# Two chunks' partial sums added at another time, another order of pairs, and earlier starts around a second MLP

## The chip, the cores and the metric

The kernel runs on one core of a Trainium2 chip. The metric is device time in microseconds (us) of one execution, lower is better. All data lie in DRAM at the start and the result is written there.

## The reference, cut to what matters

```python
def _attn_ref(q, k, v):                       # each 8 x 8 x 576 x 64 (batch, head, token, column)
    q_s = softmax(q, axis=-1)
    k_s = softmax(k, axis=2)                  # over the tokens
    kv = np.einsum('bhsd,bhse->bhde', k_s, v)
    return np.einsum('bhsd,bhde->bhse', q_s, kv)

def _moe_ref(x, w_in, w_out):                 # x 4608 x 512, w_in 512 x 2048, w_out 2048 x 512
    h = x @ w_in
    return np.maximum(0.01 * h, h) @ w_out

def _moe2_ref(x, w1, w2, w3, w_out):          # w1, w2, w3 512 x 768, w_out 768 x 512
    h = np.maximum(np.maximum(x @ w1, x @ w2), x @ w3)
    return h @ w_out

x = _attn_ref(q, k, v).transpose(0, 2, 1, 3).reshape(4608, 512)
return _moe2_ref(_moe_ref(x, ...), ...)
```

## The kernel before

**Tiling.** The 4608 tokens are nine chunks of 512 (`c`, 0 to 8). Every matrix product is made in three matmuls on a high and a low half of each operand (`ghi`/`glo`, `xhi`/`xlo`, the two halves of `op`), mostly of 128x128 weights by 512 columns. Where two chunks go together, their product with a block of weights is done in seven products of half chunks (`a11`, `a12`, `a22`, `s1` to `s4`; `s` operands are sums of quarters) where the plain way has eight.

**Stages.** From 0 to 340 us the attention of all chunks runs, and beside it the first MLP of chunks 0, 1 and 2 alone, as its weights are converted. Chunks 0 and 1 go through it in parts (`TURNS`: a chunk and a range of the sixteen blocks of `w_in`'s 2048 columns); each part leaves a partial sum of the chunk's result in DRAM, five for chunk 0 and four for chunk 1, and `join(c)` (L934) adds them up by DMAs that accumulate from DRAM to DRAM, in two halves of 512 KB for each part after the first: 14 DMAs on POOL's queue (trace name `x<-x`, L940). From 340 to about 866 us the first MLP of the pairs (3, 4), (5, 6), (7, 8) runs (`APAIRS`); the last of these goes by `inner_and_outer` (L1750), whose second layer (L1713, `acc<-opO,sumw`) uses sums of weights, `sumw`, loaded by `pair.load`. From 846 us the second MLP runs over `PAIRS`: for each pair nine units `u` (three blocks of 256 of the 768 columns by three weights; L1097, `ps<-op,group`), then a last layer (`last_layer`, L1513, with class `LastLayer`; L1453, `acc<-opL,lastw`). The pairs start at about 846, 976, 1092, 1207, and the half pair (0,) at 1321 us; that one's second layer goes the plain way with weights `wo` (L378).

**What sets the order.** The text of the kernel is a program for all engines at once; a scheduler may move what isn't pinned (`pin`), and each engine then goes through its own list in order. `background(step)` (L962) is called at steps of the main work. It starts the generators of `waiting` whose step has come (`ahead_units`, L944, a table of steps) and advances every one in `live` by a stage. `ahead_unit(u)` (L298) prepares a unit of the second MLP's first-layer weights: POOL loads `room<-in_wb_dram`, DVE and ACT make the sums and split them, POOL writes them to `stream`; `ahead_out(t)` (L342) does so for the last layer's weights, to `stream_last`. Units numbered `WIDE` and up take their rooms from another pool.

**Loads.** SP loads `group` (four of the 63 products' weights, 1 MB, L1272), `lastw` (768 KB, L1440), `wo` and the half chunks of the next pair (`raw_pair`, L1285: `side<-both` or `side<-x`), and stores the output rows (L1483). Groups, `lastw`, `wo`, sides and output rows share the 17 rooms of tag `w` of one pool, so an SP instruction waits until a room is free, and those behind it wait too.

**Last layer.** It has 21 terms `k` (seven products by three blocks of 256 rows, `LAST_TERMS`); `layer.build(k + 3)` makes the operands `opL` by ACT (high half) and DVE (low half) three terms ahead, in order of `k`; `building` makes the operands of the next pair from its sides.

Of the kernel before, what the change touches and what calls it, by code (L numbers as in the profile page):

```python
# [31 lines left out]
AHEAD_A = 2  # L32
AHEAD_OUT = 4
HELD = 2
WIDE = 7
OUT_ORDER = ("a11", "a12", "s2", "s3", "s1", "a22", "s4")

PAIRS = ((3, 4), (5, 6), (1, 2), (7, 8), (0,))
H = N // 2
USES = ("a11", "a12", "a22", "s2", "s4", "s1", "s3")  # L40
LATE = ("a22", "s4")
# [1 line left out]
AHEAD = 3  # L43
FAR_AHEAD = 6
LATE_AT = 3
RAW_AT = (3, 1)
WO_AT = (0, 1, 2)
STAGES = (0, 0, 0, 1, 1, 1, 2, 1, 1)
BUILD_AT = (8, 13)

# [30 lines left out]
def tile_kernel(ctx: ExitStack, tc: tile.TileContext, q, k, v, wa, wb, out):  # L81
# [862 lines left out]
    def ahead_units():  # L944
        for m in range(MA):
            yield max(BEGUN[m] + 7, 8), stage_a(m)
        for t in range(MA // 2):
            yield (29, 34, 39, 44, 48, 52, 56, 60)[t], sums_a(t)
        for t, at in enumerate((49, 50, 51, 73, 81, 82, 83, 84)):
            yield at, sums_out(t)  # L950
        for u, at in enumerate((68, 78, 88, 98, 107, 112, 115, 119, 146)):
            yield at, ahead_unit(u, at > 100)
        for t, at in enumerate((124, 130, 137)):
            yield at, ahead_out(t)
        for c, at in enumerate((36, 34)):
            yield at, join(c)

    waiting = [u for c in range(2, NC) for u in plan_units(c)] + list(ahead_units())
    waiting.sort(key=lambda u: u[0])
# [432 lines left out]
            store_rows(r, PAIRS[p][r // 2], H + r % 2 * P, acc, last)  # L1392

    LAST_TERMS = [(name, t) for name in OUT_ORDER for t in range(MB // 2)]

    class LastLayer:


        def __init__(self, p):
            self.p, self.rooms, self.made, self.loaded, self.snaps, self.rows = p, {}, [], {}, {}, {}  # L1400

        def quarter(self, x, t):
            if t not in self.rooms:
# [7 lines left out]
        def build(self, upto):  # L1411

            while len(self.made) < min(upto, len(LAST_TERMS)):
                k = len(self.made)
                name, t = LAST_TERMS[k]
                b11, b21, b12, b22 = (self.quarter(x, t) for x in range(4))
                if name == "s1":
                    nc.vector.tensor_tensor(b12, b22, b11, op=ALU.subtract)
                if name == "a22":
                    nc.vector.tensor_tensor(b21, b21, b11, op=ALU.subtract)  # L1420
                z = {"a11": b11, "a12": b21, "s2": b11, "s3": b12, "s1": b12, "a22": b21, "s4": b22}[name]
                tags = (("ghi", "glo"), ("ghi", "glo"), ("g", "g"), ("st", "st"), ("st", "st"))[k % 5]
                hi, lo = (
                    gp.tile([P, N], F32R, tag=tag, name="opL", bufs=4 if tag == "st" else 2) for tag in tags
                )
                nc.scalar.activation(hi, z, AF.Copy)  # L1426
                nc.vector.tensor_tensor(lo, z, hi.bitcast(F32), op=ALU.subtract)  # L1427
                if name == "a12":
                    nc.vector.tensor_tensor(b11, b12, b11, op=ALU.add)
                self.made.append((hi, lo))  # L1430

        def load(self, upto):

# [79 lines left out]
    def last_layer(layer, building):  # L1513

        a, b, c = [ps_acc.tile([P, N], F32, tag="acc", name="acc") for _ in range(2)], None, None

        def term(k):
            nonlocal b, c
            name, t = LAST_TERMS[k]
            if name == "a12" and t == 0:  # L1520
                c = [psum() for _ in range(2)]
            if name == "s1" and t == 0:
                b = [ps_acc.tile([P, N], F32, tag="acc", name="acc") for _ in range(2)]
            layer.products(k, {"a12": c, "s1": b, "s4": b}.get(name, a), name in ("a11", "a12", "s1"))
            if t == MB // 2 - 1:
                layer.finish(name, a, b, c)

        for k, (name, t) in enumerate(LAST_TERMS):
            if k == LATE_AT:
                iteration(None)  # L1530
                layer.third(MB // 2 - 1)
            layer.load(OUT_ORDER.index(name) + 3)
            layer.build(k + 3)
            if k < len(LAST_TERMS) - HELD:
                term(k)
                if k % 2:
                    background_if()
            if k in BUILD_AT:
                next(building, None)
        layer.build(len(LAST_TERMS))  # L1540
        for _ in building:
            pass
        return [lambda k=k: term(k) for k in range(len(LAST_TERMS) - HELD, len(LAST_TERMS))]
# [206 lines left out]
    def inner_and_outer(i, ops, fills):  # L1750
# [6 lines left out]
        for t in range(MA // 2):  # L1757
            new = InnerUnit(i, t, ops)
            inner(new, old, pair.quarter, fills if t == 0 else ())
            old = new  # L1760
            if t and t % 2 == 0:
                pair.third(t // 2 - 1)
            if t == MA // 2 - 2:
                pair.load(1)
        pair.load(2)
        pair.build(2)
        a, b, c = [ps_acc.tile([P, N], F32, tag="acc", name="acc") for _ in range(2)], None, None
# [115 lines left out]
    for p in range(len(PAIRS)):  # L1883
# [3 lines left out]
        for u in range(NU):  # L1887
# [4 lines left out]
                fill = fills  # L1892
            if last and u in (3, 6):
                fill = [lambda q=p, t=u // 3 - 1: out_left(q, t)]
            if last and u in WO_AT:
                load_wo(WO_AT.index(u))
            iteration(Unit(p, u, ops, best, layer), *fill)
            if not last and u in (3, 6):
                layer.third(u // 3 - 1)
            if not last:  # L1900
# [5 lines left out]
                    next(building, None)  # L1906
                if u == NU - 2:
                    layer.load(1)
                    layer.build(2)
        if not last:  # L1910
            fills = last_layer(layer, building)
        ops = nxt
# [74 lines left out]
```

## Time and profile before

| | us |
|---|---|
| median of 3 runs | 1387.64 |
| lowest, highest | 1384.84, 1391.16 |
| the profiled execution, its own time | 1390.36 |
| its span, first to last instruction | 1388.6 |
| PE (matmul) busy | 1351.8 (97%) |
| DVE, ACT, POOL busy | 1007.9 (73%), 712.5 (51%), 165.1 (12%) |
| granted TensorE clock, mean | 0.994 |

The page gives busy time by engine over the whole span. Stages have different limits, so what a change is worth is read from the stage that it touches, in the engine's timeline and its waits. PE is TensorE, DVE VectorE, ACT ScalarE, POOL GpSimd and SP SyncE. The end of a matmul is modelled, so stops of PE are a little longer than shown.

### The profile page before, as it was taken

How to read it: one execution, taken by the hardware profiler on the slowest of the kernel's cores; microseconds unless marked ns; L12 is line 12 of the kernel's file. 1: busy time of each engine (PE TensorE's matmuls, PEld its weight loads, DVE VectorE, ACT ScalarE, POOL GpSimd, SP SyncE). 2: the span in 40 equal slices, each digit the busy share in tenths (PEclk: the TensorE clock that was granted, in tenths of full speed). 3: DMA queues.
4: the chain of work that ended last, by engine and by line, in shares of the span. 5: the costliest groups of instructions: out<-in, count | busy, mean ns of one | idle time of the engine just before them, and what ended most of it. 6: DMA issues, size and time to landing. Idle time of an engine off the chain costs nothing.

```text
span 1388.6 us, 18899 instructions
## 1 busy us (share of the span) xinstructions
PE 1351.8 (97%) x6638; PEld 1108.4 (80%) x6638; DVE 1007.9 (73%) x1747; ACT 712.5 (51%) x1452; POOL 165.1 (12%) x251
## 2 busy tenths in 40 slices
PE   6999999989999999999999999999999999999998
PEld 5788877768888787887888787888788888888887
DVE  9988968754897797765748898968558567756743
ACT  6755858644676765754456555435224324423422
POOL 2001212320111121210213122200000000000000
PEclk9999999989999999999999999999999999999999
DMA  8688965898899967979677988982893594396395
GB/s 305 250 317 322 332 226 183 206 190 299 301 331 363 389 249 264 351 287 375 216 261 253 327 314 322 385 334 92 269 370 126 172 393 157 101 353 243 111 310 206
DMA packets 129502, 376.81 MB, mean 271 GB/s; under 512 B 12800, under 2 KB 68352, under 8 KB 105600
## 3 DMA queue, kind: packets, MB, share of 16 engines
q1 hardware_dynamic: 109936, 304.56, 60.4%
q0 software_dynamic: 18752, 66.72, 15.4%
q10 hardware_dynamic: 720, 4.33, 0.7%
q8 instruction: 53, 0.87, 0.2%
q14 instruction: 41, 0.34, 0.1%
HBM read 285.90 MB, written 96.99 MB: 276 GB/s over the span
## 4 chain that ended last, share of the span: by engine, by line
PE 82%; DMA 7%; DVE 6%; ACT 2%; issue 2%; SPq 1%; POOL 0%; DVEq 0%; ACTq 0%; POOLq 0%
PE ps L1097 40%; PE acc L798 19%; PE ps L798 8%; PE acc L1453 7%; PE acc L1713 3%; DMA group<-stream 2%; DMA outw<-stream_out 2%; PE ps L1453 1%; PE ps L492 1%; DMA side<-x 1%; PE ps L624 1%; PE ps L1713 1%; DMA stream_in<-room 1%; DMA sumw<-stream_out 1%; DMA stream_last<-room 0%
## 5 line engine op out<-in xcount | busy, mean ns | idle before, releaser
L1097 PE MATMUL ps<-op,group 128*128 128x512 f32 (+1 forms) x1890 | 397.0, 369 | 7.6 <-DMA group<-stream 3.5
L1097 PEld LDWEIGHTS ps<-op,group 128*128 128x128 f32 x1890 | 330.4, 188 | 71.5 <-ACT snap L1336 4.7
L1097 PE MATMUL ps<-opA,group 128*128 128x512 f32 x1008 | 241.8, 391 | 0.3 <-DMA group<-stream_in 0.3
L1097 PEld LDWEIGHTS ps<-opA,group 128*128 128x128 f32 x1008 | 188.3, 188 | 40.5 <-issue 0.7
L1336 ACT ACTIVATE snap<-ps 128x512 f32<-128x512 f32 (+1 forms) x135 | 70.9, 553 | 186.4 <-PE ps L1097 181.9
L798 PE MATMUL acc<-ghi,outw 128*128 128x512 f32 x512 | 165.4, 392 | 1.0 <-ACT ghi L821 0.9
L798 PE MATMUL acc<-ghi,w 128*128 128x512 f32 x384 | 128.0, 394 | 1.7 <-ACT ghi L821 1.7
L798 PE MATMUL ps<-xhi,w 128*128 128x512 f32 x384 | 128.0, 398 | 1.1 <-ACT g L1149 0.7
L798 PEld LDWEIGHTS acc<-ghi,outw 128*128 128x128 f32 x512 | 95.4, 188 | 21.4 <-ACT ghi L821 2.0
L1356 DVE TENSOR_TENSOR snap<-snap,ps 128x512 f32<-128x512 f32 (+1 forms) x90 | 56.6, 632 | 71.8 <-ACT snap L1336 56.7
L798 PE MATMUL acc<-glo,outw 128*128 128x512 f32 x256 | 100.4, 393 | 0.5 <-DVE glo L822 0.4
L1453 PE MATMUL acc<-opL,lastw 128*128 128x512 f32 x432 | 100.6, 389 | 0.0
L1453 PEld LDWEIGHTS acc<-opL,lastw 128*128 128x128 f32 x432 | 81.0, 188 | 16.8
L1426 ACT ACTIVATE opL<-room 128x512 fp32r<-128x512 f32 x84 | 51.7, 629 | 79.7 <-DVE room L1358 41.2
L798 PEld LDWEIGHTS ps<-xhi,w 128*128 128x128 f32 x384 | 73.1, 191 | 18.1 <-ACT g L1149 1.1
L798 PEld LDWEIGHTS acc<-ghi,w 128*128 128x128 f32 x384 | 71.9, 188 | 18.1 <-ACT ghi L821 2.4
L822 DVE TENSOR_TENSOR glo<-g,ghi 128x512 fp32r<-128x512 f32 x80 | 54.8, 687 | 41.2 <-ACT ghi L821 41.0
L798 PE MATMUL ps<-xlo,w 128*128 128x512 f32 x192 | 75.8, 395 | 0.0
L798 PE MATMUL acc<-glo,w 128*128 128x512 f32 x192 | 75.4, 393 | 0.0
L1427 DVE TENSOR_TENSOR opL<-room,opL 128x512 fp32r<-128x512 f32 x84 | 56.6, 685 | 20.4 <-ACT opL L1426 19.6
L1713 PE MATMUL acc<-opO,sumw 128*128 128x512 f32 x288 | 68.1, 392 | 2.0 <-DMA sumw<-stream_out 1.1
L1713 PEld LDWEIGHTS acc<-opO,sumw 128*128 128x128 f32 x288 | 53.6, 188 | 15.4 <-DVE opO L1679 2.5
(220 smaller groups left out, 2101.1 us busy)
## 6 DMA issues: line engine op xcount, KB each, us to landing
group<-stream SPq DMA_DIRECT2D x78, 1024.0 KB, 9.5
group<-stream_in SPq DMA_DIRECT2D x42, 1024.0 KB, 7.7
outw<-stream_out SPq DMA_DIRECT2D x32, 1024.0 KB, 8.8
lastw<-stream_last SPq DMA_DIRECT2D x28, 768.0 KB, 5.0
stream<-room POOLq DMA_DIRECT2D x66, 256.0 KB, 4.8
raw<-in_wa_dram SPq DMA_DIRECT2D x16, 1024.0 KB, 7.0
room<-in_wb_dram POOLq DMA_DIRECT2D x24, 512.0 KB, 7.0
x<-st SPq DMA_DIRECT2D x40, 256.0 KB, 3.3
```

The costliest lines, as they stand in the source:

```text
L492: ins = nc.tensor.matmul(acc[z, : D + 1], lhsT=ke[:, r, z], rhs=vt[:, r, h], start=r == 0, stop=r == RK - 1)
L624: nc.tensor.matmul(both(xps, c0, c1), lhsT=a, rhs=halves(y, c0, c1), start=i == 0, stop=i == 2)
L798: ins = nc.tensor.matmul(acc, lhsT=l, rhs=r, start=first and i == 0, stop=last and i == 2)
L822: nc.vector.tensor_tensor(lo[:, z], g[:, z], hi[:, z].bitcast(F32), op=ALU.subtract)
L1097: ins = nc.tensor.matmul(bank[:, : r.shape[1]], lhsT=l, rhs=r, start=fresh and first, stop=last, skip_group_check=not fresh)
L1336: nc.scalar.activation(t, bank[:, : self.n], AF.Copy)
L1356: nc.vector.tensor_tensor(snap, snap, bank, op=ALU.add)
L1426: nc.scalar.activation(hi, z, AF.Copy)
L1427: nc.vector.tensor_tensor(lo, z, hi.bitcast(F32), op=ALU.subtract)
L1453: nc.tensor.matmul(banks[f], lhsT=l, rhs=r, start=fresh and first, stop=final, skip_group_check=not fresh)
L1713: nc.tensor.matmul(banks[f], lhsT=l, rhs=r, start=fresh and first, stop=final, skip_group_check=not fresh)
```

## The change

1. The joins leave the table of `ahead_units` (steps 36 and 34). `last_layer` now puts `join(n)` in `live` when its pair is `JOIN_AT[n]`: chunk 1 in the last layer of the second pair, chunk 0 in that of the third.
2. `PAIRS` has (7, 8) third and (1, 2) fourth.
3. The last units of `ahead_units` come at other steps, the ninth (119) ahead of the three `ahead_out` (now 127, 135, 143); it was at 146. `WIDE` goes from 7 to 4.
4. `last_layer` builds `LOOK` = 4 terms ahead in the order `MADE_ORDER`, and begins with two at the last but one unit and two more at the last; at terms 7, 10 and 13 (`FETCH_AT`) it loads three more groups; the `wo` loads go from the first units of the half pair to the last layer before it (`WO_AT`).
5. The sides of the next pair are loaded at unit 0 and no longer 1 (`RAW_AT`), except in the first pair. `sumw` is loaded from unit 5 on (`SUMS_AT`).

```diff
-WIDE = 7
+WIDE = 4
-PAIRS = ((3, 4), (5, 6), (1, 2), (7, 8), (0,))
+PAIRS = ((3, 4), (5, 6), (7, 8), (1, 2), (0,))
+JOIN_AT = (2, 1)
-RAW_AT = (3, 1)
-WO_AT = (0, 1, 2)
+LOOK = 4
+RAW_AT = (3, 0)
+SUMS_AT = 5
+WO_AT = (9, 12, 15)
+FETCH_AT = (7, 10, 13)
...
-        for u, at in enumerate((68, 78, 88, 98, 107, 112, 115, 119, 146)):
+        for u, at in enumerate((68, 78, 88, 98, 103, 107, 112, 115, 119)):
             yield at, ahead_unit(u, at > 100)
-        for t, at in enumerate((124, 130, 137)):
+        for t, at in enumerate((127, 135, 143)):
             yield at, ahead_out(t)
-        for c, at in enumerate((36, 34)):
-            yield at, join(c)
...
+    MADE_ORDER = (0, 1, 3, 4, 2, *range(5, len(LAST_TERMS)))
...
-                name, t = LAST_TERMS[k]
+                name, t = LAST_TERMS[MADE_ORDER[k]]
...
-                self.made.append((hi, lo))
+                self.made[MADE_ORDER[k]] = hi, lo
...
+        live.extend(join(n) for n, p in enumerate(JOIN_AT) if p == layer.p)
...
-            layer.build(k + 3)
+            layer.build(k + LOOK if k >= LATE_AT else min(k + LOOK, MADE_ORDER.index(5)))
...
+            if k in FETCH_AT:
+                load_group(len(groups))
+            if k in WO_AT and layer.p == len(PAIRS) - 2:
+                load_wo(WO_AT.index(k))
...
-            if t == MA // 2 - 2:
-                pair.load(1)
+            pair.load(t - SUMS_AT)
...
-            if last and u in WO_AT:
-                load_wo(WO_AT.index(u))
...
-                    layer.build(2)
+                if u >= NU - 2:
+                    layer.build(2 * (u + 3 - NU))
```

What the change does on the engines is seen in their lists. On POOL, in the attention stage (250 to 310 us), the list before; `ke`, `vt`, `plain` and `qt` are loads of keys, values and queries, `ISA mx<-mx` is the maximum over partitions, and `x_1_124<-x_3_126 x2` two halves of a join:

```order
L474 ISA mx<-mx 128x128
L437 DMA ke<-in_k_dram 128x640
L940 DMA x_1_124<-x_3_126 128x1024 x2
L479 DMA plain<-in_v_dram 128x650
L546 DMA qt<-in_q_dram 128x512
L437 DMA ke<-in_k_dram 128x640
L479 DMA vt<-in_v_dram 128x650
L474 ISA mx<-mx 128x128
L940 DMA x_1_124<-x_5_128 128x1024 x2
L546 DMA qt<-in_q_dram 128x512
L940 DMA x_1_124<-x_7_130 128x1024 x2
L940 DMA x_0_123<-x_2_125 128x1024 x2
```

The joins of `x_1_124` (chunk 1) and `x_0_123` (chunk 0) stand between the loads and the maxima of the attention. On POOL now, the end of the list, which has no work of the second MLP behind it:

```order
L378 DMA stream_last<-room 128x2x256 x8
L351 DMA room<-in_wb_dram 128x512 x2
L378 DMA stream_last<-room 128x2x256 x16
L944 DMA x_1_124<-x_3_126 128x1024 x2
L944 DMA x_1_124<-x_5_128 128x1024 x2
L944 DMA x_1_124<-x_7_130 128x1024 x2
L944 DMA x_0_123<-x_2_125 128x1024 x2
L944 DMA x_0_123<-x_4_127 128x1024 x2
L944 DMA x_0_123<-x_6_129 128x1024 x2
L944 DMA x_0_123<-x_8_131 128x1024 x2
```

All fourteen joins moved there, behind the last weights that POOL writes (in the list before, `stream` writes of the ninth unit stood there). On PE, the passage from the first MLP's last outer layer (L1713, `sumw`) to the second MLP's first units (L1097, `group`), before:

```order
L1713 MATMUL acc<-opO,sumw 128x512 x204
L1097 MATMUL ps<-op,group 128x512 x7
L1713 MATMUL acc<-opO,sumw 128x512
L1097 MATMUL ps<-op,group 128x512 x11
L1713 MATMUL acc<-opO,sumw 128x512 x11
L1097 MATMUL ps<-op,group 128x512 x9
```

And on PE now, the same place:

```order
L1721 MATMUL acc<-opO,sumw 128x512 x216
L1099 MATMUL ps<-op,group 128x512 x20
L1721 MATMUL acc<-opO,sumw 128x512
L1099 MATMUL ps<-op,group 128x512
L1721 MATMUL acc<-opO,sumw 128x512 x11
```

Twelve of the outer layer's matmuls moved ahead of the first that needs a group. On SP, from the last layer of the fourth pair into the half pair, before:

```order
L1440 DMA lastw<-stream_last 128x1536 x4
L384 DMA wo<-stream_last 128x2x256 x4
L1483 DMA out_dram<-rows 32x7x128 x4
L1483 DMA out_dram<-rows 32x128 x4
L384 DMA wo<-stream_last 128x2x256 x4
L1272 DMA group<-stream 128x2048
L1483 DMA out_dram<-rows 32x8x128 x4
L1272 DMA group<-stream 128x2048
L1483 DMA out_dram<-rows 32x7x128 x4
L384 DMA wo<-stream_last 128x2x256 x4
L1272 DMA group<-stream 128x2048 x3
```

And on SP now, the same place:

```order
L1443 DMA lastw<-stream_last 128x1536 x2
L1274 DMA group<-stream 128x2048
L1443 DMA lastw<-stream_last 128x1536
L388 DMA wo<-stream_last 128x2x256 x4
L1274 DMA group<-stream 128x2048
L1443 DMA lastw<-stream_last 128x1536
L388 DMA wo<-stream_last 128x2x256 x4
L1274 DMA group<-stream 128x2048
L388 DMA wo<-stream_last 128x2x256 x4
L1486 DMA out_dram<-rows 32x128 x4
```

All `wo` loads and three groups moved ahead of the first row stores, and in between the last `lastw` loads.

## Rows read from the trace of the kernel before

**Rows 1.** The page: an engine's busy time, share of the span and instructions.

```profile
PE 1351.8 (97%) x6638; PEld 1108.4 (80%) x6638; DVE 1007.9 (73%) x1747; ACT 712.5 (51%) x1452; POOL 165.1 (12%) x251
```

**Rows 2.** PE's timeline, 267 to 293 us: start, length, line, work, idle before.

```profile
268.49 0.80 PE L492 MATMUL ps<-plain,ke 128*64 128x65 f32 x20
...
283.95 1.35 PE L492 MATMUL ps<-vt,ke 128*64 128x65 f32 x20 [7.09 <-ACT ke L481]
285.23 0.79 PE L798 MATMUL ps<-xhi,w 128*128 128x512 f32 x1
...
290.07 0.39 PE L798 MATMUL ps<-xhi,w 128*128 128x512 f32 x1
```

**Rows 3.** Busy us of each engine, PE clock, DMA share, GB/s.

```profile
284.00:290.00 6.00, 6.00 (x31) 4.90 (x32) 4.75 (x10) 4.58 (x10) 1.74 (x3) 0.50 0.95 193
```

**Rows 4.** PE's timeline in the second MLP, 976 to 1350 us.

```profile
981.19 17.97 PE L1097 MATMUL ps<-op,group 128*128 128x512 f32 x78 [0.69 <-ACT snap L1336]
999.62 56.23 PE L1097 MATMUL ps<-op,group 128*128 128x512 f32 x246 [0.45 <-DVE snap L1356]
...
1225.72 61.50 PE L1097 MATMUL ps<-op,group 128*128 128x512 f32 x270 [0.64 <-DVE snap L1356]
...
1333.13 2.39 PE L1097 MATMUL ps<-op,group 128*128 128x256 f32 x18 [0.83 <-DMA group<-stream]
...
1345.12 5.06 PE L1097 MATMUL ps<-op,group 128*128 128x256 f32 x40 [0.51 <-DMA group<-stream]
```

**Rows 5.** Timelines of DVE and ACT, 274 to 284 us.

```profile
274.18 0.69 DVE L567 TENSOR_REDUCE qmx<-qt 128x16 f32<-128x512 f32 x1 [4.89 <-DMA qt<-in_q_dram]
...
282.30 0.82 DVE L480 TENSOR_TENSOR ke<-ke,mx 128x640 f32<-128x640 f32 x1 [5.55 <-POOL mx L474]
...
283.16 0.74 ACT L481 ACTIVATE ke<-ke 128x640 f32<-128x640 f32 x1 [6.71 <-DVE ke L480]
```

**Rows 6.** POOL's timeline, 262 to 285 us.

```profile
273.55 1.64 POOL L940 DMA_DIRECT2D x<-x  x2 [2.53 <-DMA stream_in<-hi]
280.75 0.83 POOL L940 DMA_DIRECT2D x<-x  x1 [5.56 <-issue]
281.31 0.96 POOL L474 PARTITION_ALL_REDUCE mx<-mx  x1
```

**Rows 7.** DMA, 281 to 313 us: queues, and issues with us to landing.

```profile
q0 software_dynamic: 1574, 5.81, 96.8%
...
x<-x POOLq DMA_DIRECT2D x7, 512.0 KB, 7.9
```

**Rows 8.** PE's timeline, 770 to 850 us.

```profile
773.40 2.58 PE L1713 MATMUL acc<-opO,sumw 128*128 128x512 f32 x10 [0.71 <-DMA sumw<-stream_out]
...
848.17 1.85 PE L1097 MATMUL ps<-op,group 128*128 128x512 f32 x7 [2.14 <-DMA group<-stream]
```

**Rows 9.** POOL's timeline, its last work, 895 to 1000 us.

```profile
909.21 1.47 POOL L244 DMA_DIRECT2D stream<-room  x2 [1.34 <-DVE snap L1356]
```

**Rows 10.** Stretches of the first pair of the second MLP.

```profile
886.00:896.00 10.00, 10.00 (x45) 8.28 (x45) 10.00 (x19) 4.19 (x8) 2.92 (x4) 1.00 1.01 422
939.00:976.00 37.00, 37.00 (x165) 30.65 (x164) 29.44 (x48) 17.42 (x31) 0.00 (x0) 1.00 0.23 73
```

**Rows 11.** DMA issues, 866 to 940 us.

```profile
lastw<-stream_last SPq DMA_DIRECT2D x5, 768.0 KB, 8.5
```

**Rows 12.** The tile `lastw`, 866 to 980 us: count, ns, first and last start.

```profile
L1453 PE MATMUL acc<-opL,lastw x108: 389/389/389, 939.5 to 976.0; 128*128 128x512 f32 x108
...
L1440 SPq DMA_DIRECT2D lastw<-stream_last x7: 319/319/432, 917.4 to 952.0; - x7
```

**Rows 13.** ACT's timeline, 996 to 999 us.

```profile
997.61 1.15 ACT L1057 ACTIVATE op<-side 128x512 fp32r<-128x512 f32 x2 [3.25 <-DMA side<-x]
```

**Rows 14.** DVE, 645 to 695 us: the stretch, and a group of passes.

```profile
645.00:695.00 50.00, 49.40 (x214) 39.58 (x214) 36.12 (x47) 24.98 (x38) 7.32 (x11) 1.00 0.74 278
...
L282 DVE SCALAR_TENSOR_TENSOR room<-room 128x1024 f32<-128x1024 uint32 x2 | 2.4, 1224 | 0.0
```

More of the change, by code (lines that the diff above doesn't have):

```diff
@@ L1394, in tile_kernel @@
     LAST_TERMS = [(name, t) for name in OUT_ORDER for t in range(MB // 2)]
+    MADE_ORDER = (0, 1, 3, 4, 2, *range(5, len(LAST_TERMS)))
     class LastLayer:
         def __init__(self, p):
-            self.p, self.rooms, self.made, self.loaded, self.snaps, self.rows = p, {}, [], {}, {}, {}
+            self.p, self.rooms, self.made, self.loaded, self.snaps, self.rows = p, {}, {}, {}, {}, {}
         def quarter(self, x, t):
```

## The prediction

> **What bounds the kernel now.** I read the page's table of engines first. TensorE is busy 1351.8 us of a span of 1388.6 us [rows 1], so at its present rate no change can save more than the 36.8 us in which it stands, and what it loses while it runs below full speed. The reader is to look for each stop of PE in its timeline and ask what would have let it go on, and to leave the other engines alone except where they end such a stop.
>
> The largest stop is at 276.9 to 283.95 us, 7.09 us, ended by ScalarE's `ke` [rows 2]. Behind it the matmuls run slowly: the granted clock is 0.50 from 284 to 290 us [rows 3], the 1.2 GHz level. The twenty small matmuls take 1.35 us where the same twenty took 0.80 at 268.49, and the eleven 512-wide ones from 285.23 to 290.07 take 4.84 us [rows 2]. At full clock 78 of that form take 17.97 us, the last one 0.39, so one is issued each (17.97 - 0.39)/77 = 0.228 us [rows 2, 4], and eleven take 2.51. The stop therefore costs 7.09 + (1.35 - 0.80) + (4.84 - 2.51) = 10.0 us.
>
> What released it is a chain through three engines. ACT's `ke` (283.16) waited for DVE, DVE's `ke` (282.30) for 5.55 us on POOL's maximum `mx` [rows 5], and POOL's reduction of `mx` at 281.31 stands on its queue behind accumulating DMAs `x<-x`: one at 273.55 (a pair) and one at 280.75, the latter after 5.56 us idle for which the profile names no one but the issue itself [rows 6]. These are the joins. While they run the software queue holds 96.8% of the DMA engines and a join of 512 KB lands 7.9 us after its issue [rows 7].
>
> The other stops are short: 0.71 us on `sumw` and 2.14 us on a `group` in the last pair of the first MLP [rows 8]; in the second MLP 0.69 us on ScalarE's `snap` once in a pair, 0.45 and 0.64 us on DVE's `snap`, and 0.83 and 0.51 us on groups in the last half pair [rows 4].
>
> **The change part by part.**
>
> *Joins out of the attention stage.* The fourteen DMAs leave the POOL queue between 250 and 310 us, and the reduction then stands behind one `qt` load only. What is late next is the load of `qt`, for which DVE stood until 274.18, in front of `ke` on its list [rows 5]. Even if that does not land sooner, DVE was done with it 5.55 us before 282.30, at 276.75, and as long after it as now, 283.95 - 282.30 = 1.65 us, PE could go on, at 278.4; it ran out 7.09 us before 283.95, at 276.86, so the stop would be 1.5 us. With 3.7 us of all DMA engines less for each join (below) it does arrive sooner. Gain 10.0 us, bounds 8.5 and 10.0.
>
> *Joins at their new place.* The order shows them at the end of POOL's queue behind the last weights that it writes, and the last such writes are issued at 909.21 us now [rows 9]; nothing there waits for a step of the second MLP, so they run from about 910 us beside the loads of the first pair, not in the second layers of pairs 1 and 2. Nothing on POOL is behind them, and chunks 1 and 0 are read only for the fourth and the fifth of the pairs. Their cost is DMA time. In 281 to 313 us the software queue took 0.968 x 32 = 31.0 us of 16 engines for 5.81 MB [rows 7]; seven joins are 3.67 MB of it, and the other 2.14 MB at the best rate seen, 422 GB/s [rows 10], are 5.1 us, so a join costs (31.0 - 5.1)/7 = 3.7 us, and fourteen 52 us. The first layer of a pair eats a 1 MB group in 24 matmuls, 24 x 0.228 = 5.5 us, 192 GB/s; half of 422 is 211, so an even sharing still feeds it. From 939 to 976 us the engines are busy only 0.23 of the time [rows 10], 28 us are free, and three more groups of 2.5 us each are now fetched there. The loads run ahead: the first `lastw` is issued at 917.4 and used at 939.5, and the last, at 952.0, is used when the last seventh of the layer begins, 976 - 37/7 = 970.7, 18.7 us later, against a landing of 8.5 us [rows 11, 12]. If only half the engines' time is left, 8.5 becomes 17 us and still fits. I take a loss of 1 us; the ends are 0 and 10 us, the upper being three late `lastw` loads (next part).
>
> A rule of the Trainium skill speaks against this place. *DMA: Bandwidth & Descriptors*, section "Queues, rings and completion order", says that a DMA engine takes turns among the queue rows that have work, a packet at a time; its section "Issuing engines are not separate DMA queues" says that transfers interleave on the same engines whoever issued them. By that, joins on POOL's queue take up to half of the engines from SP's loads as long as both have work, so the DMA time comes back as longer landings and not as idle engines filled. The 96.8% of [rows 7] cannot show the sharing, since SP asked for little there. By the rule the place costs what is taken above, or the first rival; by that row read as a right of way it would cost the second.
>
> *Sums and inner weights of the last pair.* `sumw` is asked for a unit earlier, which removes the 0.71 us [rows 8]. The new order laid on the durations of this trace gives an estimate: the room comes free only about 1.4 us earlier, and inner groups before it get up to 19 us less lead. I take 0.7 us; bounds -1 and 2.
>
> *First group of the second MLP.* In the new order twelve more matmuls of the outer layer stand ahead of its first use, 12 x 0.228 = 2.7 us, and its room comes free no later. The wait of 2.14 us [rows 8] is covered. I take 2.1 us; bounds 0 and 3.
>
> *Sides a unit earlier, second-layer operands four ahead.* At 999.62 PE waited for DVE, which came late because ACT's `op<-side` had stood 3.25 us on the DMA of a side [rows 13]; the same kind of wait stands at 1225.72 [rows 4]. With the load one of the nine units of a first layer earlier both go: 0.45 + 0.64 = 1.1 us; bounds 0 and 1.5. The 0.69 us waits on `snap` stay: they are the seam between the last layer and the next pair's first products, which have the same order as before. The operands built four ahead make ACT and DVE run earlier in the last layer, where PE showed no wait; nothing is gained or lost.
>
> *Tail.* SP no longer has `wo` loads and blocked row stores between the groups of the half pair. The waits of 0.83 and 0.51 us go [rows 4]: 1.3 us; bounds 0 and 1.5. The stores of rows wait longer, but nothing reads them.
>
> *Weight units at other steps.* The last units' preparation moves up into 645 to 695 us. DVE is busy there 36.12 of 50 us [rows 14]; the order adds about eight passes of 1.22 us [rows 14], which makes 46 us. DVE still fits, but bunched passes may hold `glo`, on which the outer products wait. I take a loss of 1 us; bounds 0 and 4. `side` and `lastw` waits of the later pairs: 0.2, bounds 0 and 1.
>
> **The sum.** 10.0 + 0.7 + 2.1 + 1.1 + 1.3 = 15.2 us gained, 1 + 1 + 0.2 = 2.2 lost: 13.0 us less. Against the profiled execution's own 1390.36 us (its span of 1388.6 and 1.8 around it) that is 1377.4; that run lay 2.7 us above the median of the three runs, 1387.64, from which it is 1374.6. What will be compared is a median, and a stop of PE is a little longer than shown, since the ends of matmuls are modelled: I say 1374.
>
> **The rivals.** *Late last-layer weights.* The joins halve the landing of `lastw` and a fetched group goes ahead of each: 17 us and 5 for the group against 18.7 us of lead are 3.3 us late, three times, 10 us: 1384. For it: three fetched groups and fourteen joins meet in that layer. Against it: the layer has 28 us of free DMA time before. Chance 0.13.
>
> *Joins starve the first layer (slower than before).* If the joins hold the engines by 96.8% here too, as in [rows 7], SP's loads stop for 52 us. The loads are 22.1 us ahead [rows 12] and the group in use lasts 5.5, so PE stands for 52 - 27.6 = 24 us: 1398. It decides when the loads get less than about a fifth of the engines; slower than before by over 0.5% needs 21 us of the 24. Against it: SP has a backlog of its own there, which it had not in [rows 7]. Chance 0.05.
>
> *DVE becomes the bound in 645 to 695 us.* The added passes do not fit between the waits of `glo`: 4 us instead of 1, and the seams around give nothing back: 1378. Chance 0.08.
>
> *Only the joins pay.* The change does not do what it says in the second MLP: the short waits come back as others (a group that is asked for earlier has no free room, a side's room neither). Then 10.0 - 2.2 = 7.8 us: 1380. For it: 5.2 us of the sum rest on four waits that end by DMA. Chance 0.14.
>
> **How the numbers follow.** The forecast has the remaining 0.60, from 1368 to 1380. About 0.5%, 6.9 us, is what a measurement of this kernel can tell from no change, so faster means under 1380.7 and slower over 1394.6. Faster: 0.60, the crowded DVE 0.08 and half of the only-joins case 0.07, 0.75. Same: late `lastw` 0.13 and the other half 0.07, 0.20. Slower: 0.05. The low end of the range has every gain at its upper bound, 10.0 + 2 + 3 + 1.5 + 1.5 = 18, and costs at zero: 1369.6, less 3 us by which the runs shown lie below their median: 1366. The high end, 1385, takes in the late `lastw`; it leaves out the starved layer and little else.
>
> **What would show it.** Right: no stop over 2 us and no clock of 0.50 between 260 and 300 us; `x<-x` issued from about 910 us; PE without a wait from 866 to 976 us though the DMA share there rises to near 1; no waits on `sumw`, on the first `group` or on `snap` by DVE; the half pair shorter by a microsecond. Wrong: PE waits on `lastw` or `group` while `x<-x` is in flight, first of all between 910 and 1000 us (the two DMA rivals, told apart by which); waits on `glo` or `ghi` between 645 and 700 us (DVE); the reduction of `mx` still late behind something else on POOL (the first term).

## The result and the profile after

The changed kernel took 1376.69 us (median of 6 runs, 1374.40 to 1378.83) where the kernel before took 1389.22 us beside it (6 runs, 1384.84 to 1392.81): a ratio of 0.991, 95% interval 0.9888 to 0.9931, 12.5 us less. Its profiled execution spans 1374.3 us.

The stop that the prediction began with is gone. The page's engine line (busy us, share, instructions; compare [rows 1]), and two stretches of the attention stage (columns as in [rows 3]):

```profile
PE 1347.8 (98%) x6638; PEld 1107.5 (81%) x6638; DVE 1007.1 (73%) x1747; ACT 710.9 (52%) x1452; POOL 164.6 (12%) x251
```

```profile
276.00:284.00 8.00, 8.00 (x55) 6.73 (x55) 4.26 (x10) 3.50 (x7) 1.61 (x3) 1.00 0.37 118
284.00:290.00 6.00, 6.00 (x28) 4.93 (x28) 1.38 (x2) 1.67 (x3) 0.00 (x0) 1.00 0.00 0
```

PE is busy for the whole of both stretches, and the granted clock is 1.00 where it was 0.50. The DMA engines stand idle from 284 to 290 us; they were 0.95 busy. The joins went where the list of POOL said, beside the first pair's loads, but they start at 888 us and not at 910 (POOL's timeline, first and last, as in [rows 6]):

```profile
888.35 0.96 POOL L944 DMA_DIRECT2D x<-x  x1 [1.09 <-issue]
...
956.69 0.81 POOL L944 DMA_DIRECT2D x<-x  x1 [4.21 <-DMA x<-x]
```

What they did there is seen in three views. Queues and issues from 888 to 962 us (columns as in [rows 7]; compare the landing in [rows 11]), the tile `lastw` (compare [rows 12]), and PE's timeline at the end of the first pair's last layer with the clock of the stretch behind it:

```profile
q1 hardware_dynamic: 2395, 15.60, 53.5%
q0 software_dynamic: 2069, 7.49, 50.2%
...
x<-x POOLq DMA_DIRECT2D x14, 512.0 KB, 9.8
lastw<-stream_last SPq DMA_DIRECT2D x7, 768.0 KB, 16.8
```

```profile
L1456 PE MATMUL acc<-opL,lastw x108: 387/389/628, 925.7 to 965.9; 128*128 128x512 f32 x108
...
L1443 SPq DMA_DIRECT2D lastw<-stream_last x7: 319/319/320, 895.4 to 944.5; - x7
```

```profile
946.12 12.40 PE L1456 MATMUL acc<-opL,lastw 128*128 128x512 f32 x54
960.34 5.96 PE L1456 MATMUL acc<-opL,lastw 128*128 128x512 f32 x18 [1.82 <-DMA lastw<-stream_last]
966.14 4.24 PE L1099 MATMUL ps<-op,group 128*128 128x512 f32 x18
```

```profile
956.00:960.00 4.00, 2.52 (x12) 1.75 (x10) 3.72 (x7) 2.15 (x4) 0.81 (x1) 1.00 1.04 304
960.00:964.00 4.00, 3.66 (x9) 2.93 (x10) 0.47 (x1) 0.00 (x0) 0.00 (x0) 0.57 1.04 330
```

The two queues share the engines evenly, 53.5% and 50.2%; a `lastw` lands 16.8 us after its issue in the median, where it took 8.5 before (five loads; all seven 6.4); and one of them comes 1.82 us late. It is the last: issued at 944.50, wanted when the 54 matmuls ahead of its own are done, at 958.5, 14.0 us later, it lands 15.7 us after its issue (the DMA view of that issue alone):

```profile
lastw<-stream_last SPq DMA_DIRECT2D x1, 768.0 KB, 15.7
```

The eighteen matmuls behind that stop take 5.96 us where eighteen at full clock take 4.24 (the last row of PE's timeline above), at a granted clock of 0.57, close to the 1.2 GHz level (0.52 from 962 to 964 us). Between 866 and 950 us PE did not wait on a load.

The short waits, from PE's timeline (compare [rows 8] and [rows 4]):

```profile
671.21 1.19 PE L802 MATMUL acc<-ghi,outw 128*128 128x512 f32 x4 [0.52 <-ACT ghi L825]
672.93 0.50 PE L802 MATMUL acc<-glo,outw 128*128 128x512 f32 x1 [0.53 <-DVE glo L826]
```

```profile
763.22 2.56 PE L1721 MATMUL acc<-opO,sumw 128*128 128x512 f32 x10 [0.69 <-DMA sumw<-stream_out]
```

```profile
880.71 19.56 PE L1099 MATMUL ps<-op,group 128*128 128x512 f32 x85 [0.69 <-ACT snap L1338]
```

```profile
1312.43 8.90 PE L1099 MATMUL ps<-op,group 128*128 128x256 f32 x72 [0.47 <-ACT snap L1338]
...
1365.90 4.42 PE L802 MATMUL acc<-wo,h 128*128 128x512 f32 x18 [0.25 <-ACT h L1366]
```

Two new ones stand at 671 us, on ACT and DVE, one is left on `sumw`, none on the first `group`, one new one at 880.71; the waits on DVE's `snap` and on groups of the half pair are gone. Taken from the same wait in both traces (197.79 before, 197.09 after, on ACT's `g`), the gain is 9.7 us at the wait on `ghi` at 464.70 (475.13 before), 9.5 at `sumw` (763.22 and 773.40), 9.4 at the seam behind the first pair (971.07 and 981.19), 10.3 at the next two, 11.0 at that of the half pair (1312.43 and 1324.12) and 13.7 at the last wait (1365.90 and 1380.30). So it was made mostly in two places, the attention stage and the half pair; the two seams between the pairs where DVE's `snap` was late gave 0.9 and 0.7 us, and what the missing waits on the first `group` and on `opO` gave was given back by the stop on `lastw` and the one at 880.71. (The two profiled executions, 1390.36 and 1376.07 us, lie 14.3 apart, the medians 12.5.)

### The profile page after: what moved, and what is told of

Read it like the earlier page. It is cut to its first block, busy times and chain, and to the rows that moved or that the text cites. A ratio compares the mean times of both kernels' runs of the same rounds, so it can differ in the third digit from the quotient of the medians.

```text
span 1374.3 us, 18904 instructions
## 1 busy us (share of the span) xinstructions
PE 1347.8 (98%) x6638; PEld 1107.5 (81%) x6638; DVE 1007.1 (73%) x1747; ACT 710.9 (52%) x1452; POOL 164.6 (12%) x251
## 3 DMA queue, kind: packets, MB, share of 16 engines
q10 hardware_dynamic: 720, 4.33, 0.8%
## 4 chain that ended last, share of the span: by engine, by line
PE 89%; DVE 4%; DMA 3%; ACT 2%; issue 1%; SPq 0%; DVEq 0%; ACTq 0%
PE ps L1099 44%; PE acc L802 21%; PE ps L802 9%; PE acc L1456 6%; PE acc L1721 5%; PE ps L1456 1%; PE ps L628 1%; PE ps L496 1%; DMA lastw<-stream_last 1%; DMA outw<-stream_out 1%; PE ps L1721 1%; DMA spare<-in_q_dram 1%; DMA sumw<-stream_out 1%; DVE glo L826 0%; DVE opA L1060 0%
```

## The experiments

Times stand against the kernel before in the same session (medians 1390.0, 1389.5 and 1387.6 us).

**Joins left out.** What do the joins cost at their new place?

```diff
-        live.extend(join(n) for n, p in enumerate(JOIN_AT) if p == layer.p)
+        joined.update({n: x2[[turn for turn in turns if turn[0] == n][0]] for n in range(2)})
```

> The changed kernel without the fourteen joins (chunks 0 and 1 go on with their first partial sum alone, so part of the sum is left out). Theory: at their new place the joins cost about 3.5 us, namely the 1.82 us wait for a last-layer weight at 960 us and the 1.7 us by which the 18 matmuls behind it ran slower. Both go: about 1373 us, lastw landing back from 16.9 towards 8.5 us, no clock below 1.00 there. Rival: not the joins but the three fetched groups make the last-layer weights late; then the wait stays and the time is 1376 to 1377 us.

1373.06 us (0.9881, 0.9865 to 0.9897). No wait on `lastw`; the tile's landing (min/median/max) is back below that of before (4.4, 6.4, 14.6 us):

```profile
DMA to landing us min/median/max: 4.1/4.3/6.5
```

The joins cost 1376.69 - 1373.06 = 3.6 us beside the first pair (1.82 + 1.7 in the trace of the changed kernel), and the fetched groups alone make nothing late. The theory held.

**Joins back.**

```diff
+        for c, at in enumerate((36, 34)):
+            yield at, join(c)
...
-        live.extend(join(n) for n, p in enumerate(JOIN_AT) if p == layer.p)
```

> The changed kernel with the joins back at steps 36 and 34 of the table. Theory: the stop of 7.1 us at 276 us and the slow stretch behind it come back, 10.0 us, and the 3.5 us beside the first pair go: about 1383 us. Rival: the stop had another cause, which the change of the other steps removed; then no stop comes back and the time is 1373 us.

1382.52 us (0.9949, 0.9935 to 0.9963). PE's timeline, and the stretch behind the stop:

```profile
283.85 1.35 PE L496 MATMUL ps<-vt,ke 128*64 128x65 f32 x20 [6.94 <-ACT ke L485]
```

```profile
284.00:290.00 6.00, 6.00 (x36) 4.90 (x37) 4.75 (x10) 4.48 (x10) 1.92 (x3) 0.67 0.97 190
```

The stop is back with its length; against the run without joins they cost 1382.52 - 1373.06 = 9.5 us at the old place. The clock came back sooner here (0.67 against 0.50 from 284 to 290 us), which may be why this is a little under the 10.0 read before.

**Joins alone.** The kernel before with the joins in the last layers and the new order of pairs.

```diff
-PAIRS = ((3, 4), (5, 6), (1, 2), (7, 8), (0,))
+PAIRS = ((3, 4), (5, 6), (7, 8), (1, 2), (0,))
+JOIN_AT = (2, 1)
...
-        for c, at in enumerate((36, 34)):
-            yield at, join(c)
...
+        live.extend(join(n) for n, p in enumerate(JOIN_AT) if p == layer.p)
```

> The kernel before with the joins issued by the last layers and the new order of pairs, and nothing else of the change. Theory: 10.0 us gained in the attention stage, a cost of 0 to 4 us beside the first pair: 1379 to 1383 us against 1389. Rival: the joins pay only together with the earlier loads, because in the old order the last-layer weights have no lead to lose: 1385 us or more.

1389.09 us (0.9995, 0.9981 to 1.0009): nothing gained, and the rival held. The tile `lastw`, and PE's timeline:

```profile
L1439 SPq DMA_DIRECT2D lastw<-stream_last x7: 319/320/640, 909.4 to 952.3; - x7
...
DMA to landing us min/median/max: 13.5/28.5/32.0
```

```profile
943.71 5.49 PE L1452 MATMUL ps<-opL,lastw 128*128 128x512 f32 x12 [4.83 <-DMA lastw<-stream_last]
```

The first `lastw` is issued at about the time it was before, but a load now takes 28.5 us in the middle. PE stands 4.83 us, and twelve matmuls behind it take 5.49 us, 12 x 0.228 = 2.7 at full clock. The groups of the half pair and the sides are late in this trace too; it is that of the longest of the twelve executions, 1395.98 us, so its waits are at the long end.

**Steps back.** The changed kernel with the old table of steps and `WIDE`.

```diff
-WIDE = 4
+WIDE = 7
...
-        for u, at in enumerate((68, 78, 88, 98, 103, 107, 112, 115, 119)):
+        for u, at in enumerate((68, 78, 88, 98, 107, 112, 115, 119, 146)):
...
-        for t, at in enumerate((127, 135, 143)):
+        for t, at in enumerate((124, 130, 137)):
```

> The changed kernel with the steps of the table and the room rule of before (68 to 115, 119, 146; 127, 135, 143 back to 124, 130, 137; WIDE 7). Theory: it is the earlier last unit that gives the first pair its lead against the joins. Without it the last-layer weights land 28 us after their issue, as with the joins alone, PE waits some 5 us on lastw and runs slowly behind, and the 2 us wait on the first group and the waits on opO come back: 1381 to 1386 us. Rival: the earlier sides and fetches make the lead; then the time stays below 1379 us.

1390.23 us (1.0002, 0.9984 to 1.002), worse than expected. PE's timeline:

```profile
942.90 5.35 PE L1456 MATMUL ps<-opL,lastw 128*128 128x512 f32 x12 [5.08 <-DMA lastw<-stream_last]
```

```profile
968.96 4.37 PE L1456 MATMUL acc<-opL,lastw 128*128 128x512 f32 x18 [1.60 <-DMA lastw<-stream_last]
978.38 5.97 PE L1456 MATMUL acc<-opL,lastw 128*128 128x512 f32 x18 [5.05 <-DMA lastw<-stream_last]
```

```profile
L1456 PE MATMUL acc<-opL,lastw x108: 387/389/629, 930.9 to 984.0; 128*128 128x512 f32 x108
...
L1443 SPq DMA_DIRECT2D lastw<-stream_last x7: 319/320/642, 909.0 to 957.4; - x7
...
DMA to landing us min/median/max: 17.8/29.6/32.1
```

Three waits on `lastw`, 11.7 us, two of them with a slow stretch behind (this trace, too, is that of the longest execution, 1394.01 us of ten). The first load is not late: issued 21.9 us ahead of its use (909.0, 930.9), it lands in 18.9. The second is, for which PE stood from 937.8 on: issued at 910.81, 27.0 us ahead, it lands after 32.1. In the changed kernel the second one has the same 27.0 us (905.51, 932.52) and lands after 18.5. The DMA view of that issue alone and SP's largest wait from 880 to 925 us, in this run:

```profile
lastw<-stream_last SPq DMA_DIRECT2D x1, 768.0 KB, 32.1
...
SPq L1274 <- DMA stream<-room: 17.0, 3, 6.2
```

The same two in the changed kernel:

```profile
lastw<-stream_last SPq DMA_DIRECT2D x1, 768.0 KB, 18.5
...
SPq L1274 <- PE ps L1099: 27.9, 4, 11.5
```

With the old steps the groups wait until the last unit's weights are written to `stream`, and then four groups and two `lastw`, 5.8 MB, are issued within 2.8 us, from 907.99 to 910.81. At the 211 GB/s that SP's queue moved beside the joins in the changed kernel (15.60 MB in 74 us) this is 27 us of work, an estimate. With the new steps SP waits there only for rooms that PE frees one by one, and the same six loads are issued over 16 us (889.19 to 905.51). So the earlier steps let the changed kernel carry the joins beside the first pair by taking this backlog away, not by a longer lead: they are worth 13.5 us there.

**Joins held.** Two versions that make POOL wait, by a copy of one column from a tile of the second MLP ahead of the joins.

```diff
-        live.extend(join(n) for n, p in enumerate(JOIN_AT) if p == layer.p)
...
+    def hold(t):
+        if not held_back:
+            held_back.append(bp[0].tile([P, 1], F32, tag="held", name="held", bufs=1))
+        pin(nc.gpsimd.tensor_copy(held_back[0], t[:, :1]))
...
+                if name == "a11" and layer.p == 1:
+                    hold(layer.snaps["first", 0])
+                    live.append(join(1))
...
+            if p == 2 and u == 4:
+                hold(now.s)
+                live.append(join(0))
```

> The changed kernel with the joins made to wait: a copy of one column on GpSimd that reads a tile of the second pair's last layer stands ahead of chunk 1's joins (about 1044 us), one that reads a tile of the third pair's fifth unit ahead of chunk 0's (about 1126 us). Both fall where the DMA share was 0.3 to 0.6. Theory: the 3.5 us beside the first pair go and nothing takes their place: about 1373 us, as without joins. Rival: the joins end too late for the sides of the fourth and fifth pairs, which are loaded from 1073 and 1198 us, and one wait of 2 to 4 us takes the place of the other: 1376 to 1378 us.

1376.53 us (0.9904, 0.9889 to 0.992): the rival held. The last joins of chunk 1 are issued at 1071 us, SP holds the first side of the pair (1, 2) for 14.0 us until they are done, and the sides come late (SP's waits from 1060 to 1100 us, and PE's timeline; PE waits for DVE, which stood until the last side landed at 1092.86):

```profile
SPq L1298 <- DMA x<-x: 14.0, 1, 14.0
...
1094.83 5.55 PE L1099 MATMUL ps<-op,group 128*128 128x512 f32 x23 [3.22 <-DVE room L1354]
```

The second version releases chunk 1 by the sixth unit of the second pair:

```diff
+            if (p, u) in ((1, 5), (2, 4)):
+                hold(now.s)
+                live.append(join(2 - p))
```

> The changed kernel with the joins held as in the held one, but chunk 1's released by the sixth unit of the second pair (about 1011 us, done by about 1045) and chunk 0's by the fifth unit of the third pair, as there. Theory: the 3.2 us wait for the sides of the pair (1, 2) at 1095 us was all that stood against holding them; now neither first pair nor sides wait: about 1373 us, the time without joins. Rival: the joins beside the second pair's own loads only move the wait to a group or lastw there: 1375 to 1378 us.

1372.66 us (0.9875, 0.9859 to 0.9891), the time without joins, and the fastest kernel here. The tile `lastw` in the first pair, and the queues while chunk 0's joins run in the third (1119 to 1160 us):

```profile
DMA to landing us min/median/max: 4.1/4.2/6.4
```

```profile
q0 software_dynamic: 1140, 4.16, 52.0%
q1 hardware_dynamic: 1242, 7.95, 50.1%
...
lastw<-stream_last SPq DMA_DIRECT2D x4, 768.0 KB, 11.3
```

The joins take half of the engines here as well and `lastw` lands 11.3 us after its issue, but PE waits for none. So it is not the sharing itself that costs, but the place.

**Steps back, joins held.** Are the steps worth anything but room for the joins?

```diff
-WIDE = 4
+WIDE = 7
...
+            if (p, u) in ((1, 5), (2, 4)):
+                hold(now.s)
+                live.append(join(2 - p))
```

(with the old table of steps, as above)

> The steps of the table and the room rule of before, as in the run with steps back, but with the joins held as in the run that held them earlier. Theory: the new steps are worth 13.5 us only because the joins run beside the first pair; without that they are worth the wait on the first group (2.4 us), the two on opO (0.6) and the short ones ahead of sumw (1.0): 1376 to 1379 us. Rival: the steps carry those 13.5 us by themselves, then 1385 us or more.

1374.12 us (0.9894, 0.9866 to 0.9921), faster than either expected. The four combinations, in us and as a ratio to the kernel before, with the landing of the second `lastw` of the first pair, which has a lead of 26.8 to 27.0 us in all four:

| | joins behind the last weights | joins held |
|---|---|---|
| old steps | 1390.23 (1.0002), landing 32.1 | 1374.12 (0.9894), landing 14.4 |
| new steps | 1376.69 (0.9910), landing 18.5 | 1372.66 (0.9875), landing 4.1 |

The steps are worth 13.5 us with the joins beside the first pair and 1.5 us, which this measurement can hardly tell from nothing (the two intervals overlap), without. The burst of the old steps or the joins alone leave that load in time; both together do not. The wait on the first `group`, 2.14 us before, is not there in this run's trace, though PE has the old order of that place; with steps back it was 2.37 us, with the joins alone 1.68 and in the next run 0.42. In none of the nine traces with the new steps is it there. So the old order has it more or less by the execution.

**Joins alone, held.** The kernel before with the new order of pairs and the joins held in the same way.

```diff
-PAIRS = ((3, 4), (5, 6), (1, 2), (7, 8), (0,))
+PAIRS = ((3, 4), (5, 6), (7, 8), (1, 2), (0,))
...
-        for c, at in enumerate((36, 34)):
-            yield at, join(c)
...
+            if (p, u) in ((1, 5), (2, 4)):
+                hold(now.s)
+                live.append(join(2 - p))
```

> The kernel before with the new order of pairs and the joins held to the second and third pair, and nothing else. Theory: taking the joins off the attention stage is worth 10.0 us by itself, which the joins alone gave back beside the first pair: 1379 to 1380 us. Rival: they cost as much in the later pairs, where the sides are loaded later and the tail is tight: 1385 us or more.

1380.06 us (0.9941, 0.992 to 0.9962) where the kernel before took 1387.57: 7.5 us gained, as the theory had it, with 10 in the attention stage. The rest goes in the half pair (PE's timeline; its first two waits on groups, compare [rows 4]):

```profile
1320.31 3.12 PE L1095 MATMUL ps<-op,group 128*128 128x256 f32 x24 [1.02 <-DMA group<-stream]
1325.76 3.01 PE L1095 MATMUL ps<-op,group 128*128 128x256 f32 x18 [2.33 <-DMA group<-stream]
```

From the seam to the last wait it takes 1369.93 - 1311.11 = 58.8 us (56.2 before, 53.5 in the changed kernel). With the other edits but the steps, above, it is 1374.12: they are worth 5.9 us, and the half pair's loads are most of that.

**Loads back.** The changed kernel without `FETCH_AT`, and `wo` at the half pair's units.

```diff
-            if k in FETCH_AT:
-                load_group(len(groups))
-            if k in WO_AT and layer.p == len(PAIRS) - 2:
-                load_wo(WO_AT.index(k))
...
+            if last and u in WO_AT:
+                load_wo(WO_AT.index(u))
```

> The changed kernel without the three groups fetched in each last layer and with the wo loads back in the half pair's first three units. Theory: these loads are what made the half pair 2.7 us shorter (53.5 us from its wait on snap to its last one, 56.2 before): 2 to 3 us come back at the end, and since no group goes ahead of the last-layer weights any more, the 1.8 us wait at 960 us may shrink: 1376 to 1379 us. Rival: the half pair's gain comes from the earlier sides and operands; then its length stays at 53.5 us.

1377.12 us (0.9911, 0.9893 to 0.9929). The sum is that of the changed kernel, but it is made otherwise:

```profile
1325.73 3.85 PE L1099 MATMUL ps<-op,group 128*128 128x256 f32 x18 [2.33 <-DMA group<-stream]
```

```profile
750.17 6.18 PE L1099 MATMUL ps<-opA,group 128*128 128x512 f32 x26 [2.56 <-DMA group<-stream_in]
```

The half pair takes 1369.88 - 1311.89 = 58.0 us, 4.5 more, with a stop of 2.33 us on a group and slow matmuls behind it (eighteen in 3.85 us; 2.39 in [rows 4]); the wait on `lastw` at 960 us is not there; and a stop of 2.56 us on an inner group stands at 750 us. SP's list is the same as the changed kernel's up to there, so that stop isn't the edit's, but differs from one execution to another; why stays open. The tile `lastw` shows why the wait is gone, though the joins run as before:

```profile
L1443 SPq DMA_DIRECT2D lastw<-stream_last x7: 319/320/320, 898.5 to 941.3; - x7
...
DMA to landing us min/median/max: 12.6/17.8/19.9
```

The loads land as late as in the changed kernel, but the last one, with no fetched group ahead of it on SP, is issued 20.3 us ahead of its use (941.3, 961.6) and not 14.0. So the stop at 960 us takes both the joins and the fetched groups: these gain 4.5 us in the half pair and, while the joins run beside the first pair, cost the 3.5 at 960. The theory held for the half pair; the sum of the run, with the stop at 750 in its trace, does not show the balance.

**Sides back, operands back, sums earlier.** Three small ones.

```diff
-RAW_AT = (3, 0)
+RAW_AT = (3, 1)
```

> The changed kernel with the sides loaded at unit 1 again. Theory: the two waits of PE on DVE's snap, 0.45 and 0.64 us, come back, at the start of the second and the fourth pair, perhaps more where the joins' first pair is crowded: 1377.5 to 1379 us. Rival: the other loads' new order had removed them, 1376.5 us.

```diff
-LOOK = 4
+LOOK = 3
...
-    MADE_ORDER = (0, 1, 3, 4, 2, *range(5, len(LAST_TERMS)))
+    MADE_ORDER = tuple(range(len(LAST_TERMS)))
...
-            layer.build(k + LOOK if k >= LATE_AT else min(k + LOOK, MADE_ORDER.index(5)))
+            layer.build(k + LOOK)
...
-                if u >= NU - 2:
-                    layer.build(2 * (u + 3 - NU))
+                    layer.build(2)
```

> The changed kernel with the last layer's operands built three ahead in their old order. Theory: PE waited for none of them before, so nothing changes: 1376 to 1377.5 us. Rival: with the joins and the fetched groups in the last layer they were needed, and PE waits on opL: 1379 us or more.

```diff
-SUMS_AT = 5
+SUMS_AT = 4
```

(on the kernel with the joins held earlier)

> The one with the joins held earlier, and sumw asked for from the fourth unit on. Theory: the wait on sumw at 764 us (1.16 us there) goes: 1371.5 to 1372.5 us, at the edge of what can be measured, so the wait itself decides. Rival: sumw has no free room earlier, or takes the inner groups' rooms, and a wait on a group takes its place: 1372.5 to 1375 us.

PE's timeline of the three, in this order:

```profile
984.76 5.54 PE L1099 MATMUL ps<-op,group 128*128 128x512 f32 x16 [3.08 <-DVE snap L1358]
```

```profile
959.53 4.33 PE L1456 MATMUL acc<-opL,lastw 128*128 128x512 f32 x18 [0.98 <-DMA lastw<-stream_last]
```

```profile
750.33 7.31 PE L1099 MATMUL ps<-opA,group 128*128 128x512 f32 x24 [2.38 <-DMA group<-stream_in]
759.60 7.09 PE L1099 MATMUL ps<-opA,group 128*128 128x512 f32 x30 [1.96 <-DMA group<-stream_in]
```

Sides back: 1378.9 us (0.9924, 0.9904 to 0.9943), 2.2 us more than the changed kernel, with the wait on DVE's `snap` back at the second pair, now 3.08 us with sixteen matmuls in 5.54 us behind it (3.8 at full clock), and one of 0.75 us at the third. The intervals overlap, and the stop on `lastw` is smaller in this trace (1.34 us, no slow stretch), so it is the waits that show what the sides are worth, more than the medians do. Operands back: 1374.84 us (0.9899, 0.9871 to 0.9927); below both expectations, but its interval and the changed kernel's overlap; no wait on `opL`, and the trace has a shorter wait on `lastw`, 0.98 us and no slow stretch behind it (eighteen matmuls in 4.33 us), with the same list on SP. That wait is on the edge, so nothing is shown for the operands either way. Sums earlier: 1379.96 us (0.993, 0.9904 to 0.9955), 7.3 us slower than with the joins held earlier alone; the wait on `sumw` is gone, and two on inner groups, 2.38 and 1.96 us, with two on DVE behind them, have taken its place. The rival held.

## Why the prediction was right, and where it was not

*The bound and the first term* held: 10.0 us predicted, 9.5 by taking the joins back, 9.7 by the traces at 464.70. The stop went to nothing and the clock stayed at its upper level.

*The joins at their new place* were mis-sized: 1 us taken, 3.6 found. The working behind it held in its main step, the even sharing: SP's queue moved 15.60 MB in the 74 us from 888 to 962, 211 GB/s, the half of 422 that the prediction had. (That the queues take turns is also what the Trainium skill says in *DMA: Bandwidth & Descriptors*, "Queues, rings and completion order"; the trace agrees, with 50.2% and 53.5%.) That `lastw` landed 16.8 us after its issue where 17 was worked out is luck: 17 was twice the 8.5 us of the trace before, and without the joins the same loads land in 4.3, so the joins made it four times as long. What failed is the step to "still fits", which set 17 us against the lead of the old order, 18.7 (20.3 by PE's own times). In the new order the last load stands behind a fetched group and has 14.0 us; it landed after 15.7, 1.82 us of stop and 1.7 behind it. Each alone leaves it in time: without the joins it lands in 6.5 us, without the fetched groups it has 20.3 us of lead. The first rival had this mechanism, a group ahead of each load, and priced it for three loads; it was there for one. The cost of a join was too high, 3.7 us of all engines; 0.502 x 74 = 37.1 us for fourteen is 2.7. The prediction had divided all the time that the queue held from 281 to 313 us by the joins that were issued in it; why the queue held more for each of them there was not tried.

*The steps* were taken as a cost of 1 us on DVE. The cost is there: 0.52 us on ACT's `ghi` and 0.53 on DVE's `glo` at 671 us, in all nine traces with the new steps and in none with the old; the 0.69 us on ACT's `snap` at 880.71, which the prediction did not have, goes with the steps in the same way. But what they are for the sum was missed: with the joins where they are, they decide between 1376.69 and 1390.23 us. The prediction read the leads of `lastw`, 22.1 and 18.7 us, from the trace before and held them against a doubled landing; it did not ask what stands ahead of a load in its own queue. With the old steps that is a burst of groups, and with the joins beside it the second load lands after 32.1 us against 27.0 of lead; with the new steps it has the same lead and lands after 18.5.

*The first group*: the wait is gone in the trace after and in every other with the new steps; but with the old steps and the old order of PE it is anything from nothing to 2.37 us, so the twelve matmuls ahead of it, the step's reason, are not shown to be what covers it.

*Sums*: 0.69 us is left of the waits ahead of `sumw`, which were 0.71 and two smaller ones. The gain of 0.7 fits, but the edit isn't shown to make it: with steps back the edit is in and the waits are as before (0.47 on a group, 0.51 and 0.71 on `sumw`), and with the joins held besides (0.40, 0.50, 0.71). The danger that the prediction named, less lead for the inner groups, is what asking earlier still brings: 7.3 us.

*Sides*: 1.1 us predicted, both waits on DVE's `snap` gone, 1.6 us by the traces at the two places, 2.2 by taking the edit back.

*The tail*: 1.3 us predicted, 2.7 found from the seam to the last wait. Beside the two waits on groups one of 0.45 us on ACT's `h` went with them. Taken back, the loads cost 4.5 us there: without them a stop on a group is long enough for a slow stretch.

The sum came out at 12.5 us against 13.0 because the joins' cost, 2.6 us more than taken, stands against the tail's gain, 1.4 us more, and the sides', 0.5 to 1.1 more. That is luck of the sum and no merit of its terms. Of the signs that were named, two came out otherwise: the joins start at 888 us and not at 910, and PE does wait between 866 and 976. No rival with a price of its own happened as a whole; the first one happened at a third of its price.

## What to carry to other kernels

Traffic that is taken off one stage goes to another: look for where its queue lets it run, which is where its engine's list is free, not where the program's text calls for it; and if that place is wrong, hold it there by a small dependence. Compare the lead of every load in the new place (issue to first use) with its landing when half of the engines are left and its own queue has a backlog, and take both from the new order: here the last load lost 6 us of lead to a group put ahead of it. Edits that look independent may carry each other: here the joins alone gained nothing, the new steps gained 1.5 us where the joins were out of their way, and 13.5 us where they were not.

## What the runs showed of the hardware that I had not expected

A stop of PE of about 2 us may or may not be followed by a slow stretch: 1.82 us at 960 us was (clock 0.57), 2.14 us before ([rows 8], seven matmuls in 1.85 us, clock 1.00) was not, nor 1.96 us in the run with sums earlier (thirty in 7.09 us), nor even 2.56 us in the run with the loads back (twenty-six in 6.18 us, clock 1.00 from 750 to 756), while 2.38 us with sums earlier was (twenty-four in 7.31 us, clock 0.50, the 1.2 GHz level, from 752 to 754). Two stops of nearly the same length, 1.82 and 1.96 us, thus differ by 1.7 us in what they cost; what decides stays open.
